# The 96 leftover rows of F in `w2 h` leave the seven-product scheme and become two steps of stacked and row-tiled matmuls

## The chip, the cores and the metric

The kernel runs on one core of one Trainium2 chip. The metric is device time in microseconds (us) of one execution; the number for the kernel before is the median of three timed runs. The engines are TensorE (PE, with its weight loads shown apart as PEld), VectorE (DVE), ScalarE (ACT), GpSimd (POOL) and SyncE (SP); SP and POOL here only issue transfers.

## The reference

Two branches work on the same `x` of 2048 rows by 512 columns, and a gate per row mixes them:

```
a  = x @ Wd_re.T ;  b = x @ Wd_im.T          # DFT along the 512 columns
A  = Ws_re @ a - Ws_im @ b                   # DFT along the 2048 rows, real part
h  = silu(x @ w1) * (x @ w3)                 # w1, w3: 512 x 1376
B  = h @ w2                                  # w2: 1376 x 512
g  = sigmoid(sum(x * gate_w, -1))            # one number per row
out = g * A + (1 - g) * B
```

F = 1376 is ten chunks of 128 rows and 96 rows over. The change concerns only `h @ w2` and those 96 rows.

## The kernel before

Every value is held as two float32r parts, a high part (a copy rounded by ACT, `high`, line 107) and a low part (the rest, by DVE, `low`, line 110). A product is three matmuls, high by high, high by low and low by high (`mm3`, line 124; all matmuls are issued at line 122 and move 512 columns).

The large products are written in a Strassen-Winograd form: a 2 by 2 block product is made of seven products P1 to P7 instead of eight, of sums of blocks. The moving operand's blocks are B11, B12, B21, B22, the sums T1 to T4 (`CHAIN`, line 656).

**Order of the work.** First the products with w1, w3 and the gate (tiles X, Y, Z). From 206 us on a list of steps runs (`STEPS`, line 663), one at a time: four F blocks (the DFT along the rows, one for each 512 of them), two H blocks (`h @ w2`, for 1024 rows each), and two Y blocks (the DFT along the columns, and the output). A block runs through P1, P5, P6, P3, P7, P2, P4; a product has `NQ` steps q, four in F, three in H, two in Y. A step takes two K chunks for each of two 128-row halves r of the output, so 2 x 2 x 3 = 12 matmuls.

**The H blocks.** The eleven chunks of F stand in pairs, chunk p with chunk p + 5 (six pairs, `NP2`); the last pair is chunk 10, which holds the 96 rows, and nothing. Step q takes pairs 2q and 2q + 1. So in q = 2 the second pair has data only in its first member: B21, B22 and T4 have no second chunk there (`cols`, line 690, gives 512 columns instead of 1024), and those three steps have 6 matmuls. The four steps with B11, T1, T2 and T3 have 12, with 96 rows of data and 32 rows that are zero but for a gate row in the chunk's second half. One H block has 4 x 36 + 3 x 30 = 234 matmuls.

**Results.** P1, P6, P7 and P4 are added up in one pair of PSUM banks, P5 and P3 in another, P2 alone in a third (`step`, line 911). After P1, P5, P6 and P7 ACT copies the banks to SBUF (`read`, line 964, tiles zs, zp, zu, zu); after P3, P7, P2 and P4 DVE adds, multiplies by the gate (`spill`, line 849), and POOL stores.

**What feeds a step.** When step m has been issued, `advance` (line 739) loads blocks for step m + 8, makes the sum for step m + 4 on DVE, and splits step m + 3 (ACT the high part, DVE the low part) into one of four buffers `zo`. Loads wait on SP, in order, until a buffer of 1024 columns (`F4`, thirteen of them) is free. The parts of w2 (H_0 to H_5) are made early or, the last two pairs, in the second F block (`late`, line 1026) and stored to DRAM (`w2sp`), from where SP loads them shortly before they are needed (`load_forms`).

Of the kernel before, what the change touches and what calls it, by code (L numbers as in the profile page):

```python
# [32 lines left out]
def fnet_swiglu_gate_kernel(  # L33
# [56 lines left out]
    def take(places, shape, dtype, name):  # L90
        p, tag = at = places.pop(0)
        t = p.tile(shape, dtype, tag=tag, name=name)
        HELD[id(t)] = t, places, at
        return t

    def wide(name):
        return take(F4, [P, 1024], F32, name)

    def parts(name):
        return take(ZO, [P, 2, 4, 256], F32R, name)  # L100

    def free(*tiles):
        for t in tiles:
            _, places, at = HELD.pop(id(t))
            places.append(at)

    def high(hi, src):
        nc.scalar.activation(hi, src, AF.Copy)  # L108

    def low(hi, lo, src):  # L110
        nc.vector.tensor_sub(lo, src, hi.bitcast(F32))  # L111

    def split(hi, lo, src):
        high(hi, src)
        low(hi, lo, src)
# [5 lines left out]
    def matmul(ps, u, v, some=slice(None), **kw):  # L121
        nc.tensor.matmul(ps.rearrange("p (n a) -> p n a", a=2), u, turns(v)[:, some], **kw)  # L122
# [10 lines left out]
    gsp, ngsp = (dram.tile([2, P, 1024], F32, tag=k, name=k) for k in ("gsp", "ngsp"))  # L133
    dsp = [dram.tile([KD, P, 2, n, 256], F32, tag=f"dsp{n}", name=f"dsp{n}") for n in (4, 3)]
    w2sp = [dram.tile([NP2, P, 2, n, 256], F32, tag=f"w2sp{n}", name=f"w2sp{n}") for n in (4, 3)]
    wbsp = dram.tile([NC, P, 2, 4, 256], F32, tag="wbsp", name="wbsp")
    zsp = dram.tile([4 * NTB * P, 1024], F32, tag="zsp", name="zsp")

# [502 lines left out]
    for k in range(LOOK + 2):  # L641
# [18 lines left out]
    KIND = "F" * NTB + "HHYY"  # L660
    ORDER = [CHAIN] * (NB - 1) + [tuple(CHAIN[i] for i in (0, 5, 1, 2, 3, 4, 6))]
    NQ = [{"F": NG // 2, "H": NP2 // 2, "Y": KD // 2}[k] for k in KIND]
    STEPS = [(blk, q, k, form) for blk, nq in enumerate(NQ) for k, form in ORDER[blk]
             for q in range(nq)]
    START = [sum(NQ[:blk]) * len(CHAIN) for blk in range(NB + 1)]

    NEED = [(("B11", 0, 0), ("B12", 1, 1), ("B22", 2, 1), ("B21", 5, 0))] * (NB - 1)
    NEED.append((("B11", 0, 0), ("B21", 1, 0), ("B12", 2, 1), ("B22", 3, 1)))
# [21 lines left out]

    def cols(blk, q, form):

        return 512 if KIND[blk] == "H" and q == NQ[blk] - 1 and form in ("B21", "B22", "T4") else 1024

    def done(m, j):
        blk, q, k, form = STEPS[m]
        b = DONE[j].get(form)
        if b:
            free(RAW.pop((blk, b, q)))

    def sum_c(m):


        if not 0 <= m < len(STEPS):
            return
        blk, q, k, form = STEPS[m]
        b = {"T1": "B11", "T2": "B22", "T4": "B21"}.get(form)
        if b:
            n = cols(blk, q, b)
            t = RAW[blk, PLACE[form], q][:, :n]  # L710
            nc.vector.tensor_add(t, t, RAW[blk, b, q][:, :n])  # L711
        elif form == "T3":
            t = RAW[blk, "B11", q]
            nc.vector.tensor_sub(t, RAW[blk, "B12", q], t)  # L714
        done(m, 0)

    def split_c(m, parts_of=(0, 1)):
        if not 0 <= m < len(STEPS):
            return
        blk, q, k, form = STEPS[m]  # L720
        src = RAW[blk, PLACE.get(form, form), q]
        if 0 in parts_of:
            ZT[m] = parts(f"zo{m}")
        t = ZT[m].rearrange("p h a n -> p h (a n)")
        n = cols(blk, q, form)
        if 0 in parts_of:
            high(t[:, 0, :n], src[:, :n])
        if 1 in parts_of:
            low(t[:, 0, :n], t[:, 1, :n], src[:, :n])
            done(m, 1)  # L730
# [112 lines left out]
    def late_free(i, j):  # L843
        free(*LATE[i][2 + j])

    XB, ZB, YB = ((4, 5), (6, 7)), (0, 2), (3, 1)
    U = {}

# [54 lines left out]
    def load_forms(kind, j, p, sp, k):  # L903
# [4 lines left out]
        STAT[kind][j].append(t)  # L908
        nc.sync.dma_start(t.bitcast(F32), sp[j][p])

    def step(m):
        blk, q, k, form = STEPS[m]
        kind = KIND[blk]
        if q == 0 and k == "P6" and kind != "Y":
            load_gate(blk)
        if blk == NB - 1 and k == "P7" and q == 0:
            nb = other[blk, RESULT[k]][0]
            nc.vector.tensor_add(flat(U["p5"]), flat(U["p5"]), nb)
            free(nb)
        if q == 0 and k in ("P1", "P5", "P2"):  # L920
            banks = {"P1": XB[blk % 2], "P5": ZB, "P2": YB}[k]
            U[k] = [bank(b, f"{k}_{blk}_{r}") for r, b in enumerate(banks)]
        ps = U[{"P6": "P1", "P7": "P1", "P4": "P1", "P3": "P5"}.get(k, k)]
        zt = ZT.pop(m)
        z = zt.rearrange("p h a n -> p h (a n)")
        own = k in ("P1", "P5", "P2")
        first = k in ("P1", "P5", "P6", "P3")
        ws = STAT[kind][0 if first else 1]
        steps = [(q, z)]
        if m >= len(STEPS) - 2:  # L930
            LAST.append((q, z))
            steps = LAST if m == len(STEPS) - 1 else []
        ni = cols(blk, q, form) // 512
        f = FORMS[kind][k]
        final = blk == NB - 1 and k == "P4"
        if final and steps:
            FINAL[1] = bank(XB[1 - blk % 2][0], "P4left")

        def banks_of(r):

            if r == 0 or not final:
                return [(ps[r], slice(None), own)]
            return [(FINAL[1][:, :256], slice(0, 128), True), (ps[1][:, 256:], slice(128, 256), False)]

        for r in range(2):
            sl = slice(r * P, (r + 1) * P)
            for dst, some, new in banks_of(r) if steps else ():
                for n, zn in steps:
                    for i in range(ni):
                        w = ws[2 * n + i]  # L950
                        b = slice(i * 512, (i + 1) * 512)
                        mm3(dst, w[:, 0, f, sl], w[:, 1, f, sl], zn[:, 0, b], zn[:, 1, b],
                            new and n == 0 and i == 0, n == NQ[blk] - 1 and i == ni - 1, not new,
                            some)
        free(zt)
        advance(m)
        if q < NQ[blk] - 1:
            return

        def res(name):  # L960
            U[name] = ut.tile([P, 2, 512], F32, tag=name, name=f"z{name}_{blk}")
            return U[name]

        def read(name):
            res(name)
            for r in range(2):
                nc.scalar.activation(U[name][:, r], ps[r], AF.Copy)  # L967

        def plus(name):
            for r in range(2):  # L970
                nc.vector.tensor_add(U[name][:, r], U[name][:, r], ps[r])

        if k == "P1":
            read("s1")
        elif k == "P5":
            read("p5")
        elif k == "P6":
            read("u2")
        elif k == "P3":
            def result():  # L980
                plus("u2")
                spill(blk, 2, U["u2"])

            result() if blk else todo.setdefault(m + 3, []).append((result, ()))
        elif k == "P7" and blk == NB - 1:
            o = other.pop((blk, RESULT[k]))[1]
            nb = other[blk, RESULT["P4"]][0].rearrange("p (r n) -> p r n", r=2)
            p5, u3 = U["p5"], res("u3")
            nc.scalar.activation(u3[:, 0], ps[0], AF.Copy)
            for r, v in enumerate((u3[:, 0], ps[1])):  # L990
                nc.vector.tensor_add(p5[:, r], p5[:, r], v)
                nc.sync.dma_start(o[:, r], p5[:, r])
            nc.vector.tensor_add(nb[:, 1, :256], nb[:, 1, :256], ps[1][:, :256])
            nc.vector.tensor_add(ps[1][:, 256:], ps[1][:, 256:], nb[:, 1, 256:])
        elif k == "P7":
            read("u3")
            nc.vector.tensor_add(flat(U["p5"]), flat(U["p5"]), flat(U["u3"]))
            spill(blk, 3, U["p5"])
        elif k == "P2":
            plus("s1")  # L1000
            spill(blk, 0, U["s1"])
        else:
            spill(blk, 1, res("c21"), ps)
# [3 lines left out]
    def at(blk, n, f, *a):  # L1007
        todo.setdefault(START[blk] + n, []).append((f, a))

# [17 lines left out]
    for i, (src, sp, p) in enumerate(late):  # L1027
        blk, b = 1 + i // 3, i % 3
        n = (10, 17, 24)[b]
        at(blk, n - (5, 5, 6)[b], late_load, i, src[p], ("u3", "u3", "u2")[b])  # L1030
        at(blk, n, late_sums, i)
        at(blk, n + 1, late_split1, i)
        at(blk, n + 2, late_split2, i)
        for j in range(2):
            at(blk, n + 2 + j, late_store, i, j, sp[j][p])
            at(blk, n + 4 + j, late_free, i, j)
    for p in range(NP2):
        at(NTB, p - 3 * NQ[0], load_forms, "H", 0, p, w2sp, p)
        at(NTB, p + 1, load_forms, "H", 1, p, w2sp, p)
    nh = 3 * NQ[NTB]  # L1040
    for p in range(KD):
        early = p < NG - NP2
# [76 lines left out]
```

## Time and profile before

| | us |
|---|---|
| median of three runs | 676.71 (676.39 to 676.78) |
| the profiled execution | 675.5 |
| its span, first to last instruction | 673.7 |
| PE busy in it | 669.4 |
| the list of steps begins | 206.66 |
| the two H blocks, first to last matmul start | 496.7 to 597.5 |

The profile shows one execution. A matmul has a duration of 379 ns in it, but matmuls overlap: the distance from one start to the next is what counts, and is found by dividing a stretch by the number in it. In a row of the timeline the first number is the start, the second the length. In a row of a window the engines' busy time stands with the number of instructions in brackets.

### The profile page before, as it was taken

What the parts mean: (1) busy time and instruction counts of PE and PEld (TensorE: products, weight loads), DVE (VectorE), ACT (ScalarE), POOL (GpSimd) and SP (SyncE); (2) the same over time, 40 slices, a digit from 0 to 9 for tenths busy, and PEclk for the clock granted to TensorE, in tenths of its full rate; (3) what the DMA queues carried; (4) which work ended last, traced back from release to release, by engine and by line L of the source; (5) the groups of instructions that cost most, each with busy time, mean ns of one, the idle gap of its engine ahead of it and who ended that gap; (6) DMA issues with size and microseconds to landing.
All of it is one profiled execution on the core that took longest, in us unless ns stands there. A gap on an engine that the chain in (4) does not pass through costs nothing.

```text
span 673.7 us, 8669 instructions
## 1 busy us (share of the span) xinstructions
PE 669.4 (99%) x3101; PEld 583.1 (87%) x3101; DVE 601.6 (89%) x748; ACT 371.9 (55%) x496; POOL 64.5 (10%) x119
## 2 busy tenths in 40 slices
PE   9999999999999999999999999999999999999998
PEld 6888888888888888888888888888888888888887
DVE  6999988887779999978999899978896897898996
ACT  6765666655547764465554654554445455455451
POOL 0012112221110000001110101100000000000000
PEclk9999999999999999999999999999999999999999
DMA  7576657599998676715696279919996772874942
GB/s 280 208 293 249 229 200 266 194 357 356 423 418 317 224 216 223 293 63 205 229 386 242 90 252 349 367 57 348 391 341 235 286 259 86 312 277 157 338 134 93
DMA packets 45563, 172.54 MB, mean 256 GB/s; under 512 B 5328, under 2 KB 5712, under 8 KB 41680
## 3 DMA queue, kind: packets, MB, share of 16 engines
q1 hardware_dynamic: 32480, 118.11, 49.0%
q0 software_dynamic: 12752, 53.49, 20.1%
q8 instruction: 24, 0.39, 0.2%
q10 hardware_dynamic: 288, 0.39, 0.2%
q14 instruction: 19, 0.16, 0.1%
HBM read 114.82 MB, written 57.16 MB: 255 GB/s over the span
## 4 chain that ended last, share of the span: by engine, by line
PE 98%; DMA 1%; ACT 0%; DVE 0%; SPq 0%; issue 0%
PE P L122 68%; PE X L122 16%; PE Z L122 8%; PE Y L122 4%; PE C L122 2%; DMA xs_B<-xt 1%; DMA out<-zc 0%; DVE zc L869 0%; ACT xo L108 0%; SPq L241 0%; ACT zc L876 0%
## 5 line engine op out<-in xcount | busy, mean ns | idle before, releaser
L122 PE MATMUL P<-zo,a 128*128 128x512 f32 x1344 | 290.4, 379 | 0.0
L108 ACT ACTIVATE zo<-B 128x1024 fp32r<-128x1024 f32 (+1 forms) x182 | 188.3, 1041 | 176.1 <-PE P L122 79.4
L122 PEld LDWEIGHTS P<-zo,a 128*128 128x128 f32 x1344 | 253.8, 189 | 36.4 <-DVE zo L111 0.4
L111 DVE TENSOR_TENSOR zo<-B,zo 128x1024 fp32r<-128x1024 f32 (+1 forms) x182 | 217.7, 1203 | 29.4 <-ACT zo L108 28.9
L122 PE MATMUL P<-zo,H 128*128 128x512 f32 x468 | 101.2, 379 | 0.0
L122 PEld LDWEIGHTS P<-zo,H 128*128 128x128 f32 x468 | 88.5, 189 | 12.6
L711 DVE TENSOR_TENSOR B<-B,B 128x1024 f32<-128x1024 f32 (+1 forms) x78 | 93.0, 1192 | 0.1
L122 PE MATMUL X<-xo,wb 128*128 128x512 f32 x378 | 88.6, 379 | 0.0
L122 PEld LDWEIGHTS X<-xo,wb 128*128 128x128 f32 x378 | 71.4, 189 | 10.2
L122 PE MATMUL P<-zo,Y 128*128 128x512 f32 (+1 forms) x336 | 71.6, 375 | 0.0
L122 PEld LDWEIGHTS P<-zo,Y 128*128 128x128 f32 x336 | 62.7, 189 | 8.7
L714 DVE TENSOR_TENSOR B<-B,B 128x1024 f32<-128x1024 f32 x26 | 31.7, 1220 | 0.0
L347 POOL DMA_DIRECT2D hsp<-h x40 | 21.7, 544 | 101.4 <-DVE h L407 70.9
L122 PE MATMUL X<-xo,wa 128*128 128x512 f32 x126 | 30.6, 379 | 0.0
L122 PE MATMUL Y<-xo,wa 128*128 128x512 f32 x126 | 30.6, 379 | 0.0
L122 PE MATMUL Z<-xo,wb 128*128 128x512 f32 x126 | 30.6, 379 | 0.0
L122 PE MATMUL Z<-xo,wa 128*128 128x512 f32 x126 | 30.6, 379 | 0.0
L122 PEld LDWEIGHTS X<-xo,wa 128*128 128x128 f32 x126 | 23.8, 189 | 3.4
L122 PEld LDWEIGHTS Y<-xo,wa 128*128 128x128 f32 x126 | 23.8, 189 | 3.4
L122 PEld LDWEIGHTS Z<-xo,wb 128*128 128x128 f32 x126 | 23.8, 189 | 3.4
L122 PEld LDWEIGHTS Z<-xo,wa 128*128 128x128 f32 x126 | 23.8, 189 | 3.4
L967 ACT ACTIVATE zu<-P 128x512 f32<-128x512 f32 x30 | 17.7, 596 | 15.1 <-PE P L122 12.7
(147 smaller groups left out, 552.8 us busy)
## 6 DMA issues: line engine op xcount, KB each, us to landing
B<-cc SPq DMA_DIRECT2D x64, 512.0 KB, 5.8
hsp<-h POOLq DMA_DIRECT2D x40, 256.0 KB, 4.1
B<-hsp SPq DMA_DIRECT2D x20, 512.0 KB, 5.5
wbsp<-wb POOLq DMA_DIRECT2D x8, 1024.0 KB, 4.3
wb<-wbsp SPq DMA_DIRECT2D x8, 1024.0 KB, 7.6
B<-zsp SPq DMA_DIRECT2D x16, 512.0 KB, 8.5
H<-w2sp SPq DMA_DIRECT2D x6, 1024.0 KB, 9.5
ws<-w SPq DMA_DIRECT2D x11, 512.0 KB, 5.0
```

Of the source, the lines that this page charges most:

```text
L108: nc.scalar.activation(hi, src, AF.Copy)
L111: nc.vector.tensor_sub(lo, src, hi.bitcast(F32))
L122: nc.tensor.matmul(ps.rearrange("p (n a) -> p n a", a=2), u, turns(v)[:, some], **kw)
L347: nc.gpsimd.dma_start(hsp[g, b + k, j // 2, :, j % 2 * 512 : (j % 2 + 1) * 512], h)
L711: nc.vector.tensor_add(t, t, RAW[blk, b, q][:, :n])
L714: nc.vector.tensor_sub(t, RAW[blk, "B12", q], t)
L967: nc.scalar.activation(U[name][:, r], ps[r], AF.Copy)
```

## The change

The last pair (chunk 10 and nothing) is taken out of the seven products: in q = 2 every step of an H block has 512 columns, thus 6 matmuls (`cols`). An H block then has 7 x 30 = 210 of them. The 96 rows get two steps of their own per H block, L1 behind the first step of P3 and L2 behind the first step of P2.

A step L adds, for each of four tiles of the output (the two banks of P5 or P2 and the two of P1), two full matmuls and one that uses 32 of the 128 partitions. The three parts of the product, 3 x 96 = 288 rows of K, are stacked to 128 + 128 + 32: the first full matmul has the 96 high rows and 32 low rows of w2, the second the same high rows against the low part of h and 32 other low rows, and the last 32 low rows stand in a 32 row matmul. The four 32 row matmuls lie on four different strips of partitions (0 to 31, 32 to 63, and so on) and write to four different banks. So L1 and L2 have 8 + 4 = 12 matmuls each, and the whole program has 3101 as before: 48 full ones are taken away, 32 full ones and 16 of 32 rows are added.

For it, w2's last rows are split once (`left_split`, in the second F block in place of the sums and splits of that pair) and stored stacked (`left_store`, eight stores on POOL instead of four), and loaded as one tile of 9 x 128 columns in two transfers (`load_left_forms`), instead of H_5 in two. In each H block eight small SP loads bring the rows of h into three F4 buffers, copied to the strips where they are needed (`load_left`, before the block's step 2), a fourth F4 buffer holds the 32 row operands, and `split_left` makes the parts.

```diff
+    LEFT = {"P3": "L1", "P2": "L2"}
+    STEPS = []
+    for blk, nq in enumerate(NQ):
+        for k, form in ORDER[blk]:
+            for q in range(nq):
+                STEPS.append((blk, q, k, form))
+                if KIND[blk] == "H" and q == 0 and k in LEFT:
+                    STEPS.append((blk, 0, LEFT[k], LEFT[k]))
...
-        return 512 if KIND[blk] == "H" and q == NQ[blk] - 1 and form in ("B21", "B22", "T4") else 1024
+        return 512 if KIND[blk] == "H" and q == NQ[blk] - 1 else 1024
...
+    def load_left(blk):
+        a, b, c = RL[blk] = [wide(f"left{blk}_{v}") for v in "abc"]
+        h = hsp[blk - NTB, :2, NP2 // 2 - 1, :, 512:].rearrange("k p n -> p k n")
+        for t, to, rows in ((a, 0, slice(0, 64)), (a, 64, slice(64, 96)), (a, 96, slice(64, 96)), (b, 96, slice(0, 32)),
+                            *((c, to, slice(32, 64)) for to in range(0, P, 32))):
+            n = rows.stop - rows.start
+            nc.sync.dma_start(t[to : to + n].rearrange("p (k n) -> p k n", k=2), h[rows])
+
+    def split_left(m):
...
+        if k == "L1":
+            E = RL[blk, "e"] = take(F4, [P, 1024], F32R, f"left{blk}_e")
+            nc.scalar.activation(z[:, 0, one], a[:, two], AF.Copy, scale=-1.0)
+            nc.scalar.activation(z[q, 0, two], b[q, two], AF.Copy, scale=-1.0)
+            nc.scalar.activation(E[:, one], c[:, two], AF.Copy, scale=-1.0)
+            nc.vector.scalar_tensor_tensor(z[:96, 0, two], a[:96, two], -1.0,
+                                           z[:96, 0, one].bitcast(F32),
+                                           op0=ALU.mult, op1=ALU.subtract)
+            for n, (t, rows, to) in enumerate(((a, slice(0, P), two), (b, q, two), (c, h, one))):
+                todo.setdefault(m + n, []).append(
+                    (nc.vector.tensor_add, (t[rows, to], t[rows, one], t[rows, two])))
+            return
+        for j, v in enumerate((one, two)):
+            high(z[:, j, one], a[:, v])
+            high(z[q, j, two], b[q, v])
+        high(RL[blk, "e"][:, two], c[:, one])
+        for j, v in enumerate((one, two)):
+            low(z[:96, j, one], z[:96, j, two], a[:96, v])
...
+    def left_store(i):
+        t = LATE[i][2].bitcast(F32)
+        hi, lo = t[:, :512], t[:, 512:]
+        for to, n, rows in ((0, lo, slice(64, 96)), (1, lo, slice(0, 32))):
+            b = slice(to * 512, to * 512 + 512)
+            nc.gpsimd.dma_start(w2l[:96, b], hi[:96])
+            nc.gpsimd.dma_start(w2l[96:, b], n[rows])
+        for g, b in enumerate((256, 384, 0, 128)):
+            nc.gpsimd.dma_start(w2l[32 * g : 32 * g + 32, 1024:], lo[32:64, b : b + P])
...
+    def left_step(m):
+        blk, _, k, _ = STEPS[m]
+        w = STAT["L"]
+        z = ZT[m].rearrange("p h a n -> p h (a n)")
+        e = RL[blk, "e"][:, 512 * (k == "L2") :][:, :512]
+        banks = U["P5" if k == "L1" else "P2"] + U["P1"]
+        for n in range(2):
+            for g, ps in enumerate(banks):
+                b = 512 * n + (256, 384, 0, 128)[g]
+                matmul(ps, w[:, b : b + P], z[:, g // 2 * (k == "L2"), 512 * n : 512 * n + 512],
+                       start=False, stop=False, skip_group_check=True)
+        for g, ps in enumerate(banks):
+            rows = slice(32 * g, 32 * g + 32)
+            matmul(ps, w[rows, 8 * P :], e[rows], start=False, stop=False, skip_group_check=True)
...
+        if (src, p) == (w2, NP2 - 1):
+            at(blk, n, left_split, i)
+            at(blk, n + 1, left_store, i)
+            at(blk, n + 5, lambda i=i: free(LATE[i][2]))
+            continue
...
-    for p in range(NP2):
+    for p in range(NP2 - 1):
         at(NTB, p - 3 * NQ[0], load_forms, "H", 0, p, w2sp, p)
         at(NTB, p + 1, load_forms, "H", 1, p, w2sp, p)
+    at(NTB, NP2 - 1 - 3 * NQ[0], load_left_forms)
+    for blk in (NTB, NTB + 1):
+        at(blk, 2, load_left, blk)
```

On TensorE, in the first H block, the steps q = 0 and q = 2 of P3 stand like this before (zo is the split moving operand, H_0 to H_5 the parts of w2, P_4_0_4267 and P_4_1_4268 the banks of P5 and P3; one row is the three matmuls of a product):

```order
L122 MATMUL P_4_0_4267<-zo_4341,H_0_3975 128x512 x3
L122 MATMUL P_4_0_4267<-zo_4341,H_1_3992 128x512 x3
L122 MATMUL P_4_1_4268<-zo_4341,H_0_3975 128x512 x3
L122 MATMUL P_4_1_4268<-zo_4341,H_1_3992 128x512 x3
L122 MATMUL P_4_0_4267<-zo_4358,H_2_4009 128x512 x3
```

And now (P_4_0_4265 and P_4_1_4266 are the banks of P5 and P3, P_4_0_4201 and P_4_1_4202 those of P1; left_forms are the stacked rows of w2, left_e the 32 row operands):

```order
L122 MATMUL P_4_1_4266<-zo_4331,H_1_3984 128x512 x3
L122 MATMUL P_4_0_4265<-zo_4348,left_forms 128x512
L122 MATMUL P_4_1_4266<-zo_4348,left_forms 128x512
L122 MATMUL P_4_0_4201<-zo_4348,left_forms 128x512
L122 MATMUL P_4_1_4202<-zo_4348,left_forms 128x512
L122 MATMUL P_4_0_4265<-zo_4348,left_forms 128x512
L122 MATMUL P_4_1_4266<-zo_4348,left_forms 128x512
L122 MATMUL P_4_0_4201<-zo_4348,left_forms 128x512
L122 MATMUL P_4_1_4202<-zo_4348,left_forms 128x512
L122 MATMUL P_4_0_4265<-left_e,left_forms 128x512
L122 MATMUL P_4_1_4266<-left_e,left_forms 128x512
L122 MATMUL P_4_0_4201<-left_e,left_forms 128x512
```

Step L1 has come in between the first and the second step of P3, and it writes to the banks of P1 too, which ACT must have read by then.

On VectorE, in the same block, this stood between the split of P2's first step and the split of P4's first step (B are the loaded blocks and their sums, zp and zu results, zo_4506 the split for P4):

```order
L111 TENSOR_TENSOR zo_4459<-B_4_1_4373,zo_4459 128x1024
L711 TENSOR_TENSOR B_4_0_4106<-B_4_0_4106,B_4_0_4356 128x1024
L111 TENSOR_TENSOR zo_4477<-B_4_2_4394,zo_4477 128x512
L997 TENSOR_TENSOR zp_4_4320<-zp_4_4320,zu_4_4480 128x1024
L857 TENSOR_TENSOR zp_4_4320<-zp_4_4320,gate_1_4327 128x512 x2
L711 TENSOR_TENSOR B_4_1_4124<-B_4_1_4124,B_4_1_4373 128x1024
L111 TENSOR_TENSOR zo_4506<-B_4_0_4106,zo_4506 128x1024
```

Now the same place reads (zo_4462 is L2's operand, zo_4525 the split for P4):

```order
L111 TENSOR_TENSOR zo_4462<-left_a,zo_4462 96x512 x2
L111 TENSOR_TENSOR zo_4478<-B_4_1_4378,zo_4478 128x1024
L1094 TENSOR_TENSOR zp_4_4312<-zp_4_4312,zu_4_4481 128x1024
L925 TENSOR_TENSOR zp_4_4312<-zp_4_4312,gate_1_4317 128x512 x2
L760 TENSOR_TENSOR B_4_0_4099<-B_4_0_4099,B_4_0_4346 128x1024
L111 TENSOR_TENSOR zo_4505<-B_4_2_4397,zo_4505 128x512
L760 TENSOR_TENSOR B_4_1_4117<-B_4_1_4117,B_4_1_4378 128x1024
L111 TENSOR_TENSOR zo_4525<-B_4_0_4099,zo_4525 128x1024
```

The two low parts of L2 are new in front, and the addition that waits for ACT's copy of P7 (zp with zu) now stands ahead of both sums and of the split of P2's last step.

On ScalarE, before, P2's first and second step were split one right behind the other:

```order
L108 ACTIVATE zo_4442<-B_4_0_4356 128x1024
L108 ACTIVATE zo_4459<-B_4_1_4373 128x1024
L108 ACTIVATE zo_4477<-B_4_2_4394 128x512
L967 ACTIVATE zu_4_4480<-P_4_0_4208 128x512
L967 ACTIVATE zu_4_4480<-P_4_1_4209 128x512
```

Now L2's five copies stand between them, and the copies of P7 come right behind the second step's split:

```order
L108 ACTIVATE zo_4447<-B_4_0_4346 128x1024
L108 ACTIVATE zo_4462<-left_a 128x512
L108 ACTIVATE zo_4462<-left_b 32x512
L108 ACTIVATE zo_4462<-left_a 128x512
L108 ACTIVATE zo_4462<-left_b 32x512
L108 ACTIVATE left_e<-left_c 128x512
L108 ACTIVATE zo_4478<-B_4_1_4378 128x1024
L1064 ACTIVATE zu_4_4481<-P_4_0_4201 128x512
L1064 ACTIVATE zu_4_4481<-P_4_1_4202 128x512
```

The work that stands ahead of P7's copies on ScalarE has grown by five copies, and shrunk by the split of P2's last step.

More of the change, by code (lines that the diff above doesn't have):

```diff
@@ L135, in fnet_swiglu_gate_kernel @@
     w2sp = [dram.tile([NP2, P, 2, n, 256], F32, tag=f"w2sp{n}", name=f"w2sp{n}") for n in (4, 3)]
+    w2l = dram.tile([P, 9 * P], F32, tag="w2l", name="w2l")
     wbsp = dram.tile([NC, P, 2, 4, 256], F32, tag="wbsp", name="wbsp")
@@ L662, in fnet_swiglu_gate_kernel @@
     NQ = [{"F": NG // 2, "H": NP2 // 2, "Y": KD // 2}[k] for k in KIND]
-    STEPS = [(blk, q, k, form) for blk, nq in enumerate(NQ) for k, form in ORDER[blk]
-             for q in range(nq)]
-    START = [sum(NQ[:blk]) * len(CHAIN) for blk in range(NB + 1)]
+    LEFT = {"P3": "L1", "P2": "L2"}
[6 more added lines that the diff above has]
+                    STEPS.append((blk, 0, LEFT[k], LEFT[k]))
+    START = [next(m for m, v in enumerate(STEPS) if v[0] == blk) for blk in range(NB)]
     NEED = [(("B11", 0, 0), ("B12", 1, 1), ("B22", 2, 1), ("B21", 5, 0))] * (NB - 1)
@@ L699, in done @@
             free(RAW.pop((blk, b, q)))
+    RL = {}
+    def load_left(blk):
[7 more added lines that the diff above has]
+        blk, _, k, _ = STEPS[m]
+        z = ZT[m] = parts(f"zo{m}")
+        z = z.rearrange("p h a n -> p h (a n)")
+        a, b, c = RL[blk]
+        one, two, q, h = slice(0, 512), slice(512, 1024), slice(96, 128), slice(64, 128)
+        if k == "L1":
[16 more added lines that the diff above has]
+            low(z[:96, j, one], z[:96, j, two], a[:96, v])
+        free(*RL.pop(blk))
     def sum_c(m):
@@ L706, in sum_c @@
         blk, q, k, form = STEPS[m]
+        if k[0] == "L":
+            return
         b = {"T1": "B11", "T2": "B22", "T4": "B21"}.get(form)
@@ L712, in sum_c @@
         elif form == "T3":
-            t = RAW[blk, "B11", q]
-            nc.vector.tensor_sub(t, RAW[blk, "B12", q], t)
+            n = cols(blk, q, form)
+            t = RAW[blk, "B11", q][:, :n]
+            nc.vector.tensor_sub(t, RAW[blk, "B12", q][:, :n], t)
         done(m, 0)
@@ L720, in split_c @@
         blk, q, k, form = STEPS[m]
+        if k[0] == "L":
+            return split_left(m)
         src = RAW[blk, PLACE.get(form, form), q]
@@ L844, in late_free, with left_split @@
         free(*LATE[i][2 + j])
+    def left_split(i):
+        r = LATE[i][0]
+        t = take(F4, [P, 1024], F32R, "left_w")
+        LATE[i].append(t)
+        split(t[:, :512], t[:, 512:], r[:, :512])
+    def left_store(i):
[7 more added lines that the diff above has]
+            nc.gpsimd.dma_start(w2l[32 * g : 32 * g + 32, 1024:], lo[32:64, b : b + P])
     XB, ZB, YB = ((4, 5), (6, 7)), (0, 2), (3, 1)
@@ L909, in load_forms, with load_left_forms @@
         nc.sync.dma_start(t.bitcast(F32), sp[j][p])
+    def load_left_forms():
+        t = a1.tile([P, 2, 4, 256], F32R, tag=f"a1_{NP2 - 1}", name="left_forms")
+        w = STAT["L"] = t.rearrange("p h a n -> p (h a n)")[:, : 9 * P]
+        for b in (slice(0, 1024), slice(1024, 9 * P)):
+            nc.sync.dma_start(w[:, b].bitcast(F32), w2l[:, b])
+    def left_step(m):
+        blk, _, k, _ = STEPS[m]
+        w = STAT["L"]
[10 more added lines that the diff above has]
+            matmul(ps, w[rows, 8 * P :], e[rows], start=False, stop=False, skip_group_check=True)
+        if k == "L2":
+            free(RL.pop((blk, "e")))
     def step(m):
@@ L913, in step @@
         kind = KIND[blk]
+        if k[0] == "L":
+            left_step(m)
+            free(ZT.pop(m))
+            return advance(m)
         if q == 0 and k == "P6" and kind != "Y":
```

## The prediction

> **What bounds the kernel now.** I read the page's first part, the pieces of the chain that ended last, then windows over the stretch of the step list and the matmuls of the H blocks.
>
> ```profile
> PE 669.4 (99%) x3101; PEld 583.1 (87%) x3101; DVE 601.6 (89%) x748; ACT 371.9 (55%) x496; POOL 64.5 (10%) x119
> ...
> 206.66 461.18 PE P L122 x2136
> ```
>
> The chain is one piece of TensorE from 206.66 us on. The windows (PE, PEld, DVE, ACT, POOL busy) of that stretch, of one F block and more, and of the H blocks:
>
> ```profile
> 206.66:668.00 461.34, 461.34 (x2141) 403.64 (x2140) 424.24 (x460) 245.20 (x295) 31.07 (x55) 1.00 0.67 244
> ...
> 206.66:300.00 93.34, 93.34 (x435) 81.63 (x434) 91.78 (x102) 59.57 (x77) 5.89 (x11) 1.00 0.66 231
> ...
> 496.70:597.90 101.20, 101.20 (x470) 88.62 (x469) 85.84 (x91) 49.45 (x58) 5.58 (x8) 1.00 0.68 248
> ```
>
> TensorE is busy for 461.34 of 461.34 us at granted clock 1.00: from 206.66 us on it waits for nobody. So matmul time taken from an H block shortens the end one for one, until another engine comes too late. In the F stretch DVE was busy for 91.78 of 93.34 us and TensorE still did not wait; in the H blocks DVE has 101.20 - 85.84 = 15.4 us free and ACT 51.8.
>
> ```profile
> L122 PEld LDWEIGHTS P<-zo,H x468: 189/189/189, 496.5 to 597.3; 128*128 128x128 f32 x156
> L122 PE MATMUL P<-zo,H x468: 379/379/379, 496.7 to 597.5; 128*128 128x512 f32 x156
> ```
>
> From first to last start lie 467 distances in 597.5 - 496.7 = 100.8 us: 0.216 us from matmul to matmul, though one lasts 0.379. Its weights load beside the matmul ahead.
>
> **The change, part by part: TensorE.** Each H block loses 24 full matmuls (234 to 210) and gains 16 full ones and two groups of four 32-row ones. For both blocks 48 go and 32 full come: 16 x 0.216 = 3.45 us less. Against that stand four groups. With c for the time by which a group moves the next matmul, the sum is -3.45 + 4c.
>
> No matmul before works on fewer than 128 rows, so c has to be bounded. Below: four that stream side by side take one matmul's distance, 0.216, and 4c = 0.86. Above, if they gain nothing from their separate strips: 4 x 0.216 = 0.864, and 4c = 3.45, no gain at all. The weights decide between: a group needs four loads in the time of one stream. The nearest rows are the last step's matmuls of 256 columns, which need loads faster than any others:
>
> ```profile
> 667.66 1.50 PE L122 MATMUL P4left<-zo,Y 128*128 128x256 f32 x12
> 669.00 1.50 PE L122 MATMUL P<-zo,Y 128*128 128x256 f32 x12
> ```
>
> Twelve take 669.00 - 667.66 = 1.34 us, 0.112 each with its load: a load of 128 x 128 needs at most 0.112 of the array's time. Of the four loads two fit under the last full matmul ahead (0.216); two are left, and if one of them lies beside the first strips' streams, c is one stream and one load, 0.216 + 0.112 = 0.33. I take that: nearer to side by side, since the strips share neither rows nor banks. 4c = 1.31, and TensorE changes by -3.45 + 1.31 = **-2.14 us**.
>
> The Trainium skill ("TensorE: Matmul & The Clock Gate", Part 3) gives 3.07 times the speed for four row tiles of 32 rows by 512 columns. As an estimate from that page c is 0.864 / 3.07 = 0.28 and the sum -2.33 us; no trace here shows it.
>
> **DVE and ACT in the H blocks.** Their groups there by shape (mean ns of one behind the busy time):
>
> ```profile
> L111 DVE TENSOR_TENSOR zo<-B,zo 128x1024 fp32r<-128x1024 f32 x35 | 42.5, 1222 | 13.4 <-ACT zo L108 13.4
> L711 DVE TENSOR_TENSOR B<-B,B 128x1024 f32<-128x1024 f32 x14 | 17.1, 1220 | 0.0
> ...
> L111 DVE TENSOR_TENSOR zo<-B,zo 128x512 fp32r<-128x512 f32 x6 | 4.1, 685 | 0.0
> ...
> L108 ACT ACTIVATE zo<-B 128x1024 fp32r<-128x1024 f32 x36 | 38.0, 1055 | 37.6 <-PE P L122 17.5 <-DVE B L711 13.1 <-issue 7.1
> ...
> L108 ACT ACTIVATE zo<-B 128x512 fp32r<-128x512 f32 x6 | 3.8, 630 | 7.3 <-PE P L122 5.9 <-DVE B L711 1.4
> ```
>
> Per block DVE halves four low parts and two sums, 6 x (1.22 - 0.685) = 3.2 us less, and gets six operations of 512 columns, 6 x 0.685 = 4.1: 0.9 more. ACT halves four copies, 4 x (1.055 - 0.63) = 1.7 less, and gets eight, 5.0: 3.3 more. (Fewer partitions I count at the same price; an upper bound.) That fits into 15.4 and 51.8 us free, if it comes in time.
>
> The tight place is the second L step. Count from the end of P7's q = 1. A buffer zo comes free when the step four places earlier ends, so ACT starts L2's five copies 2.59 (12 x 0.216) earlier and ends at 5 x 0.63 - 2.59 = 0.56; P2's second split lasts to 1.62. P7 ends at 6 x 0.216 = 1.30, so ACT can read its two banks until about 2.82 (0.60 each, in the ACT rows below). L2 writes the first of them after P2's first step and two matmuls, at 1.30 + 2.59 + 0.43 = 4.32, the second at 4.53: 1.7 us to spare.
>
> Behind that read stands DVE's addition, with the split of P4's first step behind it. Here is the same stretch before, first ACT, then DVE:
>
> ```profile
> 534.48 0.60 ACT L967 ACTIVATE zu<-P 128x512 f32<-128x512 f32 x1 [0.70 <-PE P L122]
> ...
> 535.11 1.22 DVE L997 TENSOR_TENSOR zp<-zp,zu 128x1024 f32<-128x1024 f32 x1 [0.92 <-ACT zu L967]
> 536.37 1.29 DVE L857 TENSOR_TENSOR zp<-zp,gate 128x512 f32<-128x512 f32 x2
> 537.58 1.22 DVE L711 TENSOR_TENSOR B<-B,B 128x1024 f32<-128x1024 f32 x1
> 538.71 1.22 DVE L111 TENSOR_TENSOR zo<-B,zo 128x1024 fp32r<-128x1024 f32 x1
> 539.85 0.69 DVE L711 TENSOR_TENSOR B<-B,B 128x512 f32<-128x512 f32 x1
> 540.45 1.82 DVE L111 TENSOR_TENSOR zo<-B,zo 128x1024 fp32r<-128x1024 f32 x2
> ```
>
> From start to start 1024 columns take 1.13 (537.58 to 538.71), 512 take 0.60, the pair with the gate 1.21. In the new order DVE starts the addition at 2.82; then come addition (1.13 to 1.26), gate pair, sum, split of 512, sum, split for P4: 2.82 + 1.2 + 1.21 + 1.13 + 0.6 + 1.13 + 1.22 = 9.3. TensorE needs that low part with P4's second matmul: P7's end 1.30, P2's first step 2.59, L2 8 x 0.216 + 0.33 = 2.06, then 2.59, 1.30 and 0.22, which is 10.06. So 0.75 us are left; what is late next, should anything slip, is this split. I cost DVE and ACT at nothing.
>
> **Transfers and queues.** SP's loads of the parts of w2 (min/median/max ns of one), a row of SP's waits from 440 to 600 us (total, times, longest), and a store on POOL in the second F block:
>
> ```profile
> L909 SPq DMA_DIRECT2D H<-w2sp x12: 319/324/1400, 457.4 to 494.3; - x12
> ...
> SPq L737 <- DVE zo L111: 45.3, 13, 18.3
> ...
> 335.28 0.53 POOL L859 DMA_DIRECT2D zsp<-zp  x1 [5.30 <-DVE zp L857]
> ```
>
> SP issues eight more loads per H block, 8 x 0.324 = 2.6 us, ahead of the last parts of w2 for P2, the gates and B21 for P2, all needed 15 us or more later; two transfers of H_5 go. Loads already wait on SP for free buffers (longest 18.3 us) without TensorE noticing, since each is asked for eight steps ahead; four of the thirteen buffers are now held in an H block for up to 16 steps, so that margin shrinks. POOL issues eight stores instead of four, at 0.53 each 2.1 us more, ahead of a store which before waited 5.30 us for DVE anyway. In the F block DVE and ACT lose work. Nothing of it is on the path.
>
> **Sum.** -2.14 us. The profiled execution took 675.5 (span 673.7), 1.2 below the median of the runs; on the median 676.71 that makes **674.6 us**, 0.3% less. Ends: c = 0.216 gives -3.45 + 0.86 = -2.59, 674.1; c = 0.864 gives 676.7.
>
> **Rivals.**
> - *Paced by weight loads.* If the four loads cannot lie beside each other's matmuls, a group takes 4 x 0.112 = 0.45: -3.45 + 1.79 = -1.66, 675.05. For it: loads run one matmul ahead in the trace (496.5 and 496.7), not four.
> - *Drained array.* If going to strips and back empties the array, each of eight changes shows what overlap hides now, 0.379 - 0.216 = 0.163; with side by side strips that is -2.59 + 1.30 = -1.29, 675.4. Nothing here mixes shapes of the array, so no row speaks on it. The Trainium skill states it ("TensorEngine Tiling (Array Packing)", Key Properties): a change of tiling mode drains TensorE. By that rule the gain would halve.
> - *The strips gain nothing.* Then the change does not do what it says: 48 distances go, 48 come, 676.7.
> - *Each strip waits for the one before to end.* Then a group costs 4 x 0.379 = 1.52 and the sum is -3.45 + 6.06 = +2.61, 679.3: slower. It decides from c = (3.45 + 1.35) / 4 = 1.2. Against it: no matmul in the trace does so, when it writes to another bank or to the same.
> - *The late split.* If the copies of P7, or the split for P4, come later than counted, TensorE waits once per H block. The point is 0.75 us; to be 0.2% slower it takes 0.75 + (2.14 + 1.35) / 2 = 2.5 us of delay per block, about two 1024 column operations: some 678.5. Loads kept back by the four buffers would end in the same wait. Against it: DVE's 15.4 us free.
>
> **How the numbers follow.** 0.2%, 1.35 us, is about what a measurement tells from no change. Forecast (674.1 to 674.9) 0.45; paced by loads 0.16; drained 0.10; nothing gained 0.10; each waits 0.08; late split 0.11. Faster by over 0.2% (under 675.36): the forecast, nearly all of the paced case, under half of the drained, 0.61. Slower: the last two, 0.19. Within: the rest, 0.20. The range goes from 673.9 (c at its lower bound, less 0.2 for the spread of runs) to 677.4, which takes in the gain lost and part of a stall; the slower ends, not quite 0.2, are left out.
>
> **What would show it.** Right: the four starts of a group on left_e lie within about 0.12 us, and the next full matmul follows 0.33 behind the first; TensorE is busy throughout the H blocks, which end 2.1 us earlier. Paced: starts 0.11 apart. Drained: a gap of some 0.16 before the first strip and behind the last. Wrong: starts 0.216 or 0.379 apart, or an idle time of TensorE that ends with DVE's zo at P4. The sum falls if c is far from 0.33, or if the steps of six matmuls run out of split operands.

## The result, and the profile after

The changed kernel takes 674.73 us (median of 14 runs, 674.42 to 675.51), the kernel before, in the same series, 675.75 (14 runs). The ratio is 0.9983, with a 95% interval of 0.9975 to 0.9991: about 1.15 us less, between 0.6 and 1.7. The profiled execution has a span of 673.0 us instead of 673.7.

First the chain that ended last and the windows of the changed kernel (PE, PEld, DVE, ACT, POOL busy):

```profile
206.98 460.11 PE P L122 x2136
...
206.66:667.00 460.34, 460.34 (x2139) 401.18 (x2138) 422.77 (x465) 249.70 (x308) 32.97 (x59) 1.00 0.68 242
...
496.70:597.90 101.20, 101.20 (x475) 86.89 (x475) 87.87 (x103) 55.90 (x74) 5.58 (x8) 1.00 0.75 265
```

The step list is still one piece of TensorE, which waits for nobody. It lasts 460.11 us instead of 461.18: 1.07 us less, which lies within the measured 0.6 to 1.7. DVE has 2.0 us more to do in the H window, ACT 6.4, and TensorE does not notice.

So the loss against the forecast lies in TensorE's own time. The groups of 32-row matmuls, by tile (ns min/median/max, first and last start):

```profile
L122 PEld LDWEIGHTS P<-zo,left_forms x32: 189/189/189, 518.8 to 585.6; 128*128 128x128 f32 x32
L122 PE MATMUL P<-zo,left_forms x32: 379/379/379, 519.0 to 585.8; 128*128 128x512 f32 x32
L122 PEld LDWEIGHTS P<-left_e,left_forms x16: 181/181/182, 520.8 to 586.1; 32*128 32x128 f32 x16
L122 PE MATMUL P<-left_e,left_forms x16: 478/478/479, 520.8 to 586.1; 32*128 32x512 f32 x16
```

And one group, the first, in the timeline of TensorE (start, length) and then of its weight loads. The first row is the last full matmul before the group; the third and the last, from neighbouring windows, give the starts of the first and the second full matmul behind it:

```profile
520.49 0.38 PE L122 MATMUL P<-zo,left_forms 128*128 128x512 f32 x1
520.80 0.49 PE L122 MATMUL P<-left_e,left_forms 32*128 32x512 f32 x4
521.22 0.70 PE L122 MATMUL P<-zo,H 128*128 128x512 f32 x2
...
521.53 0.59 PE L122 MATMUL P<-zo,H 128*128 128x512 f32 x2
```

```profile
520.27 0.19 PEld L122 LDWEIGHTS P<-zo,left_forms 128*128 128x128 f32 x1
520.79 0.19 PEld L122 LDWEIGHTS P<-left_e,left_forms 32*128 32x128 f32 x4 [0.33 <-issue]
521.21 0.73 PEld L122 LDWEIGHTS P<-zo,H 128*128 128x128 f32 x4 [0.23 <-issue]
```

Four strips, 478 ns each, lie within 0.49 us, so all four start within some 0.01 us: they do run side by side, and their four loads (181 ns each, 0.19 together) do too. But the load of a full matmul's weights starts 0.22 us before its matmul (520.27 and 520.49), while the strips' loads start at 520.79, together with the strips, 0.30 behind the last full matmul. The same happens on the way back: the load starts at 521.21, its matmul at 521.22, the next one 0.31 later (521.53). The ends of matmuls are modelled in a profile, so no row shows whether the array was empty in between; the rows show that the new shape's load starts 0.09 us after the next matmul would have started (0.30 against 0.216). From 520.49 to 521.53 are 1.04 us where two distances would be 0.43: a group costs **c = 0.61 us**, and -3.45 + 4 x 0.61 = -1.01 us.

### The profile page after: what moved, and what is told of

It is laid out like the page before. It is cut to its first block, busy times and chain, and to the rows that moved or that the text cites. A ratio compares the mean times of both kernels' runs of the same rounds, so it can differ in the third digit from the quotient of the medians.

```text
span 673.0 us, 8728 instructions
## 1 busy us (share of the span) xinstructions
PE 669.0 (99%) x3101; PEld 580.8 (86%) x3101; DVE 599.6 (89%) x753; ACT 376.2 (56%) x509; POOL 66.4 (10%) x123
## 4 chain that ended last, share of the span: by engine, by line
PE 99%; DMA 0%; DVE 0%; ACT 0%; issue 0%
PE P L122 68%; PE X L122 16%; PE Z L122 8%; PE Y L122 4%; PE C L122 2%; PE wps L434 1%; DMA out<-zc 0%; DVE zc L937 0%; ACT zc L944 0%
## 5 line engine op out<-in xcount | busy, mean ns | idle before, releaser
L108 ACT ACTIVATE zo<-B 128x1024 fp32r<-128x1024 f32 (+1 forms) x182 | 185.1, 1022 | 174.3 <-PE P L122 76.6
L111 DVE TENSOR_TENSOR zo<-B,zo 128x1024 fp32r<-128x1024 f32 (+1 forms) x182 | 213.0, 1177 | 29.6 <-ACT zo L108 28.9
L122 PE MATMUL P<-zo,H 128*128 128x512 f32 x420 | 91.9, 380 | 0.0
L760 DVE TENSOR_TENSOR B<-B,B 128x1024 f32<-128x1024 f32 (+1 forms) x78 | 91.7, 1175 | 0.1
L122 PEld LDWEIGHTS P<-zo,H 128*128 128x128 f32 x420 | 79.1, 189 | 12.0 <-issue 0.9
L764 DVE TENSOR_TENSOR B<-B,B 128x1024 f32<-128x1024 f32 (+1 forms) x26 | 30.6, 1177 | 0.0
L111 DVE TENSOR_TENSOR wa<-ws,wa 128x768 fp32r<-128x768 f32 (+1 forms) x22 | 19.3, 879 | 7.0 <-ACT wa L108 6.9
```

Of the source, the lines that this page charges most:

```text
L764: nc.vector.tensor_sub(t, RAW[blk, "B12", q][:, :n], t)
```

## The experiments

Theory A, formed from these rows: each change between full and 32-row matmuls costs about 0.2 us, since the weights of the other shape are loaded only when the array has run empty and nothing covers that load; the strips themselves are cheap. Theory B: the strips are slow by themselves, so that every group (or strip) costs its share of the 0.61. Theory C: a group costs the forecast 0.33, and other engines or transfers took the rest. Ratios are against the kernel before, run on the same chip.

**Without the strips.** In `left_step`:

```diff
-        for g, ps in enumerate(banks):
-            rows = slice(32 * g, 32 * g + 32)
-            matmul(ps, w[rows, 8 * P :], e[rows], start=False, stop=False, skip_group_check=True)
```

> The sixteen 32-row matmuls are left out (the output lacks one third of the small terms of 32 of the 96 rows). Theory A, change of shape: in the trace of the changed kernel a group moves TensorE's next full matmuls by 1.04 us (520.49 to 521.53) where two distances of 0.216 would be 0.43, so a group costs 0.61, all of it on TensorE. Without the groups the time falls by 4 x 0.61 = 2.4 us against the changed kernel, 3.45 against the one before (about -0.51%). Theory B, the strips themselves are slow: the same. Theory C, the missing 1.1 us of the forecast were lost to other engines or transfers and a group costs 0.33: only 1.3 us less than the changed kernel, about 2.4 less than before (-0.35%), with idle time of TensorE elsewhere.

Measured 672.17 us, ratio 0.9944 (0.993 to 0.9958). The piece of TensorE in the chain of this kernel:

```profile
206.79 457.69 PE P L122 x2120
```

It is 2.42 us shorter than the changed kernel's 460.11 and 3.49 shorter than the 461.18 before. So 16 x 0.216 = 3.45 holds, nothing else was lost anywhere, and the groups cost 2.42 / 4 = 0.61 each. C falls.

**Each group twice.**

```diff
-        for g, ps in enumerate(banks):
+        for g, ps in [*enumerate(banks)] * 2:
```

> Each group of four 32-row matmuls is issued twice, one right behind the other (the terms are added twice, so the output is off). Theory A: the change of shape is paid once per place, the second group streams behind the first for one matmul's 0.216: 4 x 0.216 = 0.86 us more than the changed kernel, about -0.2 us against before (-0.03%). Theory B: every group costs 0.61 again, 2.4 us more than the changed kernel, +1.4 against before (+0.2%).

Measured 675.52 us, ratio 0.9993 (0.9984 to 1.0001). The chain's piece and the loads of the first pair of groups:

```profile
206.94 460.97 PE P L122 x2152
```

```profile
520.75 0.30 PEld L122 LDWEIGHTS P<-left_e,left_forms 32*128 32x128 f32 x8 [0.33 <-issue]
521.39 0.30 PEld L122 LDWEIGHTS P<-zo,H 128*128 128x128 f32 x2 [0.33 <-issue]
```

460.97 is 0.86 more than 460.11: the second groups cost 0.215 each, one stream. All eight loads, two for each strip, lie within 0.30 us, and the way back starts 0.64 behind the first of them instead of 0.42. What is expensive is the change, not the group.

**One strip instead of four.**

```diff
-        for g, ps in enumerate(banks):
+        for g, ps in enumerate(banks[:1]):
```

> Of each group only the first 32-row matmul is left (terms of three of four output tiles are missing). Theory A: the switch there and back costs the same for one strip as for four, so the time is that of the changed kernel, about 1.0 us under before (-0.15%). Theory B, 0.15 us for each strip: 4 x 3 x 0.15 = 1.8 us less than the changed kernel, 2.9 under before (-0.43%).

Measured 674.55 us, ratio 0.998 (0.9972 to 0.9989). Chain and first strip:

```profile
206.79 460.06 PE P L122 x2124
```

```profile
520.60 0.48 PE L122 MATMUL P<-left_e,left_forms 32*128 32x512 f32 x1
521.01 1.56 PE L122 MATMUL P<-zo,H 128*128 128x512 f32 x6
```

One strip costs what four cost (460.06 against 460.11), 0.41 us from its start to the next full matmul. The other three are free. B falls in both forms, and so does the rival that weight loads pace a group.

**Each strip alone.** The strip g stands right behind the full matmul g of the second half:

```diff
             for g, ps in enumerate(banks):
                 b = 512 * n + (256, 384, 0, 128)[g]
                 matmul(ps, w[:, b : b + P], z[:, g // 2 * (k == "L2"), 512 * n : 512 * n + 512],
                        start=False, stop=False, skip_group_check=True)
-        for g, ps in enumerate(banks):
-            rows = slice(32 * g, 32 * g + 32)
-            matmul(ps, w[rows, 8 * P :], e[rows], start=False, stop=False, skip_group_check=True)
+                if n == 1:
+                    rows = slice(32 * g, 32 * g + 32)
+                    matmul(ps, w[rows, 8 * P :], e[rows], start=False, stop=False, skip_group_check=True)
```

> The same matmuls as the changed kernel, but each 32-row matmul stands alone between two full ones, so there are 32 switches instead of 8. Theory A: sixteen single strips at 0.61 us each, 9.8 instead of 2.4: 7.4 us more than the changed kernel, 6.4 over before (+0.9%), with about 0.3 us without a weight load ahead of each strip. Theory B: the same number of strips, the time of the changed kernel (-0.15% against before).

Measured 682.04 us, ratio 1.0102 (1.0082 to 1.0122), 7.3 us more than the changed kernel with the same matmuls. In the timeline:

```profile
521.99 0.48 PE L122 MATMUL P<-left_e,left_forms 32*128 32x512 f32 x1
522.40 0.48 PE L122 MATMUL P<-zo,left_forms 128*128 128x512 f32 x1
522.81 0.48 PE L122 MATMUL P<-left_e,left_forms 32*128 32x512 f32 x1
523.22 0.48 PE L122 MATMUL P<-zo,left_forms 128*128 128x512 f32 x1
```

```profile
522.39 0.19 PEld L122 LDWEIGHTS P<-zo,left_forms 128*128 128x128 f32 x1 [0.23 <-issue]
```

Where every matmul changes the shape, the distance is 0.41 us instead of 0.216, full or strip: a change costs 0.195. Each place now has eight changes and four streams, 8 x 0.195 + 4 x 0.216 = 2.42 us instead of 0.61, which makes 7.2 us more for the four places, where 7.3 was measured. (The profiled execution is the longest of four, 685.49 us; from 578.8 to 582.4 us its granted clock was 0.53, and the rows above lie outside that stretch.) A full matmul is shown at 0.48 too, 0.10 longer than covered ones; its own load starts with it (522.39 and 522.40). So of 0.195 about 0.10 is the load that nothing covers. About 0.09 lies before the load (0.30 from the last start to the load, less 0.216); that this is the array running empty is a reading, and how the two parts divide was not varied by itself.

**Full matmuls in place of the strips.**

```diff
-            rows = slice(32 * g, 32 * g + 32)
-            matmul(ps, w[rows, 8 * P :], e[rows], start=False, stop=False, skip_group_check=True)
+            matmul(ps, w[:, 8 * P :], e, start=False, stop=False, skip_group_check=True)
```

> The sixteen 32-row matmuls become sixteen matmuls over all 128 rows at the same places (each adds the same terms for all four strips, so the output is off). Theory A: no change of shape is left, each costs one distance, 16 x 0.216 = 3.45 us: 0.0 us against before (674.7 + 1.0 for the changed kernel's base), 1.0 more than the changed kernel, and no idle time of the weight loads around them. If instead the L steps themselves lost time (their waits, the order of the banks), this kernel is slower than the one before by that amount.

Measured 675.66 us, ratio 0.9997 (0.9988 to 1.0006): no difference from the kernel before. Chain and loads at those places:

```profile
206.82 461.10 PE P L122 x2136
```

```profile
L122 PEld LDWEIGHTS P<-left_e,left_forms x16: 189/189/189, 520.3 to 587.0; 128*128 128x128 f32 x16
L122 PE MATMUL P<-left_e,left_forms x16: 379/379/379, 520.5 to 587.2; 128*128 128x512 f32 x16
```

The loads lead their matmuls by 0.2 us again. The steps L, their waits and their order cost nothing; only the shape does.

**The cover on DVE.** One more DVE operation in each H block, behind the multiplications of P7, of 512 or of 1024 columns:

```diff
             spill(blk, 3, U["p5"])
+            if KIND[blk] == "H":
+                v = flat(U["p5"])[:, :1024]
+                nc.vector.tensor_sub(flat(U["u3"])[:, :1024], v, v)
```

> One more DVE operation of 512 columns (0.60 us from start to start) in each H block behind the multiplications by the gate of P7, ahead of the split of P4's first step. Nothing is left out. In the trace of the changed kernel that split ends 0.75 us before TensorE needs it. If the count of 0.75 us is right, 0.15 us are left and the time stays that of the changed kernel (-0.15% against before). If the cover is smaller, up to 2 x 0.6 = 1.2 us more.

> The same with 1024 columns (1.13 us). With 0.75 us of cover TensorE waits 1.13 - 0.75 = 0.38 us in each H block: 0.8 us more than the changed kernel (about -0.03% against before), with an idle time of TensorE at P4's first step that DVE's zo ends. If DVE has more room there, nothing changes.

With 512 columns 674.68 us, ratio 0.9982 (0.9973 to 0.9991), as the changed kernel. With 1024 columns 676.12 us, ratio 1.0004 (0.9995 to 1.0013): 1.4 more, where 0.8 was expected. Now DVE is in the chain of that kernel:

```profile
534.11 1.23 DVE zp L1094
...
537.84 1.22 DVE B L760
539.05 0.60 DVE zo L111
539.65 1.14 DVE B L760
540.79 1.15 DVE zo L111
541.94 0.04 issue
541.98 38.74 PE P L122 x180
```

From the addition zp to the split for P4 lie 540.71 - 534.11 = 6.60 us (the split's start is in the timeline), where the changed kernel has 5.33 and the 512 column variant 5.93. The delay is 1.27, not 1.13: the new operation, which reads what the multiplications have just written, starts 0.1 us later than operations in the row before it did. (The 512 column variant reads only the first multiplication's half and adds just its 0.60.) Less 0.75, the split is 0.52 late in each block, and TensorE, which had nothing left to do, pays for the uncovered load as well: about 0.65 in a block, 1.3 in all. The load behind the wait starts together with its matmul:

```profile
541.98 0.70 PE L122 MATMUL P<-zo,H 128*128 128x512 f32 x2 [0.39 <-DVE zo L111]
...
541.98 0.19 PEld L122 LDWEIGHTS P<-zo,H 128*128 128x128 f32 x1 [0.80 <-DVE zo L111]
```

In the changed kernel's trace the cover was as counted, and the price of falling out of it is higher than the delay.

**One place instead of two.** If a change of shape costs and strips do not, the eight strips of an H block should stand together. For that four sums must be open at one time. L1 goes behind the first and L2 behind the second step of P3; L2 opens P2's banks early, and uses the other pair of P1's banks (S) for what DVE then adds to p5:

```diff
-    LEFT = {"P3": "L1", "P2": "L2"}
+    LEFT = {0: "L1", 1: "L2"}
...
+            U["P2"], U["S"] = ([bank(b, f"{n}_{blk}_{r}") for r, b in enumerate(v)]
+                               for n, v in (("P2", YB), ("S", XB[1 - blk % 2])))
+            sets = [(U["P2"], 256, 0), (U["P1"], 0, 0), (U["S"], 0, 1)]
...
+        for v, two in enumerate((U["P5"] + U["P1"], U["P2"] + U["S"])):
+            e = RL[blk, "e"][:, 512 * v : 512 * v + 512]
+            for g, ps in enumerate(two):
+                rows = slice(32 * g, 32 * g + 32)
+                matmul(ps, w[rows, 8 * P :], e[rows], start=False, stop=v == 1 and g > 1,
+                       skip_group_check=True)
...
+                    todo.setdefault(m + AFTER, []).append((nc.vector.tensor_add, (t, t, U["S"][r])))
```

The excerpt leaves out how `split_left` is fitted to it: the sums of h's rows are formed earlier, and the 32 row operand is copied in smaller pieces, with two more copies on ACT in each H block.

> All terms are computed, with one place for the 32-row matmuls in an H block instead of two: L1 stands behind the first and L2 behind the second step of P3, L2 starts P2's banks and the other pair of P1's banks, and the eight strips of both stand together at its end; DVE adds that pair to p5. Theory A: two switches there and back fewer, each 0.61 - 0.216 = 0.40 us: 0.8 us less than the changed kernel, 1.8 less than before (-0.27%). Theory B, a price for each group: the time of the changed kernel (-0.15%). If DVE's two more additions come too late, up to 2 x 1.2 us more.

Measured 673.95 us, ratio 0.9974 (0.9964 to 0.9983). The pieces of the chain around its first group, and its last piece:

```profile
206.95 316.48 PE P L122 x1466
...
525.15 0.63 PE P L122 x6
525.78 0.01 PE S L122 x2
525.78 47.25 PE P L122 x218
...
575.39 90.86 PE P L122 x420
```

TensorE alone again, from 206.95 to 666.25: 459.30 us, 0.81 less than the changed kernel's 460.11. It is the fastest of all kernels here that compute everything, 0.26% under the kernel before; against the changed kernel the intervals of the two ratios still overlap, so there the chain is the evidence. Eight strips take 0.64 us from start to the next full matmul (0.63 and 0.01 in the chain).

## Why the prediction was right or wrong

- **What bounds the kernel.** Right. From 207 us on the time is TensorE's, before and after. Without strips, with groups doubled, with one strip and with full matmuls, the kernel's time moved as its piece in the chain did, within 0.15 us.
- **16 x 0.216 = 3.45 us.** Right: 3.49 in the trace without strips, and 0.0 when strips are made full matmuls.
- **c = 0.33.** Here it failed: 0.61 was measured. The step was that two of the four loads "fit under the last full matmul ahead" and one of the other two lies beside the first strips' streams. In its place: no load of the new shape starts until 0.30 us behind the last full matmul's start, so none fits under it; the four loads then run together (one strip costs what four do), and the way back pays the same once more. The strips did start within 0.12 us of each other, as was said, but the next full matmul followed 0.42 behind the first, not 0.33, and the one after it 0.31 later instead of 0.216. The sum is -1.01 instead of -2.14. The row I leaned on, 256 column matmuls at 0.112 each, tells how fast loads follow each other within one shape; it says nothing on a change.
- **The rivals.** Of the six ways the drained array is the one that the runs fit, at 0.10 of the chances: strips side by side, and a price for each change in both directions. Its 0.379 - 0.216 = 0.163 for a change was near the measured 0.195, though the trace shows other parts, about 0.09 before the load and about 0.10 of bare load; it gave -1.29, where the chain shows -1.07. Pacing by loads, strips that gain nothing, and strips that wait for each other's end are ruled out by the one strip, the doubled groups and the full matmuls. The Trainium skill's rule ("TensorEngine Tiling (Array Packing)", Key Properties: a change of tiling mode drains TensorE) agrees with these runs, which show 0.195 us for a change, though no row shows the array empty; I had given it too little weight because no row of the trace before showed it. The speed of 3.07 for four row tiles that the Trainium skill gives ("TensorE: Matmul & The Clock Gate", Part 3), and which by estimate made c 0.28, does not hold for a single group between full matmuls: 0.864 / 0.61 = 1.4 times. For the second of two groups in a row it is 0.864 / 0.215 = 4.0. In the late split's price there is a slip: 676.71 + 1.35 is 678.1, not 678.5; nothing hangs on it.
- **DVE and ACT at nothing.** Right, and in size: DVE got 87.87 - 85.84 = 2.0 us more (1.8 forecast), ACT 55.90 - 49.45 = 6.4 (6.6 forecast). The tight place is where it was said to be. In the changed kernel's timeline of DVE the split for P4's first step stands like this:

```profile
533.41 1.22 DVE L1094 TENSOR_TENSOR zp<-zp,zu 128x1024 f32<-128x1024 f32 x1
...
538.74 1.22 DVE L111 TENSOR_TENSOR zo<-B,zo 128x1024 fp32r<-128x1024 f32 x1
```

It ends at 539.96. P2's last two steps start behind L2 at 536.51; with the bare load and 19 distances TensorE needs it at 540.71. That is 0.75 us of cover, and the two DVE variants lie on both sides of it. It is also the number worked out beforehand, but partly by luck, since both ends of it came 0.27 us later than counted: TensorE's need by the mis-sized c of L2, and DVE's addition because ACT's copies of P7 ended later. (P7's q = 1 ends at 530.38: L2 starts at 534.27, and 3.89 before it stand P2's first step and P7's last. The split ends 9.58 behind that instead of 9.31, and is needed 10.33 behind it instead of 10.06.)
- **Transfers and queues at nothing.** Right as far as the end goes: no engine row shows TensorE waiting, and without strips nothing is missing.
- **The time.** 674.6 was forecast and 674.73 measured, but this closeness is luck: the base of 676.71 came from three runs, and 14 gave 675.75. The gain, 2.14 forecast and about 1.1 measured, was half of what was said, and the change came out within 0.2%, which had a chance of 0.20, not faster by more, which had 0.61.

## What to carry to other kernels

Count the places where a matmul's shape on the array changes, not only the matmuls (only 128 and 32 rows were run here): each change between 128-row and 32-row matmuls cost 0.195 us, almost a whole matmul of 512 columns, while four strips cost what one does, and the next four cost 0.215 us. So gather row-tiled matmuls into few places, even if that needs another pair of PSUM banks and two more additions on an engine with room. Where a term's price has no row in the trace, a rule that speaks against the change deserves more weight than a likely-looking extrapolation from rows of another situation.

## What the runs showed of the hardware that was not expected

- Between full matmuls the weights are loaded 0.2 us ahead (520.27 for the matmul at 520.49), but not across a change of shape: the load starts 0.30 us behind the last full matmul's start, or 0.42 behind the first strip's, and lies bare, in both directions.
- Loads into different strips run together: four take 0.19 us, where one takes 0.18; two for each of four strips take 0.30.
- A stall of TensorE costs more than the delay that causes it: 0.52 us of lateness became about 0.65, since the first load after it is uncovered too.
